# Attention and feed-forward in one kernel: a new written-out order for the steps after the start, another order for the first 300

## The chip, the cores and the metric

The kernel runs on one core of a Trainium2 chip. The metric is the device time of one execution in microseconds (us); "before" is the kernel as it was, "after" the changed one.

## The reference, cut to what matters

Batch 8, 12 heads, 448 rows, head width 64. The attention output, with the heads side by side, is the 3584 x 768 input of a two-layer feed-forward block of width 2048. Inputs and output are f32.

```
q_n = q / sqrt(mean(q*q) + 1e-6) * g_q          # k_n in the same way
attn = softmax(q_n @ k_n^T / 8);  x = attn @ v  # (8, 12, 448, 64) -> (3584, 768)
h = x @ w_in                                    # (3584, 2048)
out = (h * clip(h + 3, 0, 6) / 6) @ w_out       # (3584, 768)
```

## The kernel before

Two heads of one batch form a pair, and there are 48 pairs, six to a batch. For each pair the kernel loads q, k and v (`ld`, 256 KB each, from SyncE's queue; k and q of a pair go into one tile `qk`), squares q and k (`sq`, or `sqh` for half of a q), sums the squares (`red1`, `red15`, `redh`, `red2`), takes the inverse root as a logarithm and an exponential (`ln`, `ex`), scales q and k into `qks` (`sc`, or `sch` for half of a q), casts v into `va` (`cv`), transposes `qks` (`tr`, `trh` on TensorE with the copies `ck`, `cq`, `cqh`; later pairs by DMA and the scaling `kt`), multiplies for the scores (`s`), takes their exponential (`e`), multiplies by v (`av`, `avh`), divides by the row sum (`rd`, `xn`, `xnh`) and transposes the result into `xT` (`xt`, `xth` with `cx`, `cxh`, or a DMA). Batch 0 is worked in two halves of its rows, so that its first scores can start early.

When a batch's six pairs are done, its hidden columns follow: `h1`, `h3` multiply `xT` by `w_in_sb`, `relu` (ScalarE, into `ts`) and `gate` (VectorE, into `gT`) make the activation. The last product (`y384`) is done for pairs of row tiles with seven products in place of eight, for which sums and differences of `gT` (`ga`, 128 x 1024 bf16, two inputs in SBUF) and of `w_out_sb` (`wb`) are formed, and the parts of `y` are added up (`yt`, `yu`, `cy384`) and stored. The weights come in eight DMAs from GpSimd's queue: `w_in` in four column strips (strip c of four is read by the hidden columns 4c to 4c+3), `w_out` in four row strips.

The kernel doesn't run these loops as they stand. Each operation is put into a plan as a numbered step with its predecessors and the engines that may do it; the loops only make the list of 2487 steps. Two tables written out by hand then decide everything: `ORDER` lists the step numbers in the order in which they are issued, and `WAY` names, for steps that have a choice, which of their engines does it (0, the first, where it has no entry). `em` ties every instruction to the one before it on its engine, so each engine works through its own steps strictly in the order of `ORDER`, and a step whose input is late holds up all later steps of its engine.

```
for i in order:
    kind, engines, fn, preds = self.ops[i]
    fn(engines[WAY.get(i, 0)])
```

So the k-th instruction of an engine in the trace can be matched with the k-th step that `ORDER` gives to that engine; step numbers beside trace times below come from this. At line 635 and 657 stand the exponentials, at 399 and 401 the squares (ScalarE, GpSimd), at 404 the scaling by the root, at 385, 387 and 389 the copies and casts (ScalarE, VectorE, GpSimd), at 869 the sums `ga`, at 838 the sums `wb`, at 1008 the DMAs of `w_in`, at 889 the last product, at 769 the gate.

Of the kernel before, what the change touches and what calls it, by code (L numbers as in the profile page):

```python
# [24 lines left out]
    53: 1, 54: 1, 61: 1, 63: 2, 68: 1, 69: 1, 83: 1, 84: 1, 90: 2, 95: 1, 121: 1, 122: 1, 126: 1, 127: 1,  # L25
    128: 1, 145: 1, 150: 1, 151: 1, 158: 1, 160: 1, 209: 1, 215: 1, 216: 1, 227: 1, 234: 1, 245: 1, 247: 1,
    335: 1, 336: 1, 365: 2, 386: 1, 456: 1, 461: 1, 473: 1, 488: 1, 489: 1, 522: 1, 553: 1, 570: 1, 588: 2,
    605: 1, 617: 1, 623: 2, 634: 1, 636: 1, 652: 2, 663: 1, 736: 1, 779: 1, 785: 1, 796: 1, 804: 1, 805: 1,
    837: 2, 863: 1, 880: 1, 888: 1, 889: 1, 895: 2, 926: 1, 927: 1, 991: 1, 998: 1, 999: 1, 1066: 1, 1092:
    1, 1107: 2, 1118: 1, 1133: 1, 1150: 1, 1165: 2, 1185: 1, 1191: 2, 1223: 1, 1226: 1, 1230: 1, 1231: 1,  # L30
    1303: 1, 1316: 1, 1319: 1, 1320: 1, 1326: 1, 1343: 1, 1358: 1, 1377: 1, 1378: 1, 1384: 2, 1395: 1, 1404:
    1, 1427: 1, 1435: 1, 1500: 1, 1535: 1, 1536: 1, 1563: 1, 1564: 1, 1567: 1, 1572: 1, 1575: 1, 1599: 1,
    1616: 1, 1622: 2, 1639: 1, 1647: 1, 1665: 1, 1673: 1, 1680: 1, 1699: 1, 1738: 2, 1757: 1, 1764: 2, 1775:
    1, 1795: 1, 1810: 1, 1811: 1, 1839: 1, 1871: 1, 1876: 1, 1889: 1, 1899: 1, 1925: 1, 1931: 2, 1942: 1,
    1951: 1, 1957: 2, 1968: 1, 1976: 1, 1977: 1, 1983: 1, 2000: 1, 2015: 2, 2047: 1, 2071: 1, 2076: 1, 2079:
    1, 2082: 1, 2083: 1, 2103: 1, 2131: 1, 2135: 1, 2139: 1, 2143: 1, 2146: 1, 2147: 1, 2183: 1, 2212: 1,
    2219: 1, 2236: 1, 2250: 1, 2271: 1, 2325: 1, 2340: 1, 2381: 1, 2413: 1, 2421: 1, 2434: 1, 2442: 1, 2445:
    1, 2448: 1, 2453: 1, 2454: 1, 2484: 1,
# [4 lines left out]
    58, 57, 35, 68, 92, 61, 36, 59, 12, 70, 60, 29, 69, 62, 209, 15, 73, 71, 211, 64, 72, 119, 74, 240, 37,  # L43
    83, 30, 66, 210, 76, 38, 39, 118, 65, 84, 40, 75, 67, 41, 227, 85, 18, 102, 77, 104, 103, 93, 42, 94,
    79, 212, 81, 43, 222, 80, 86, 44, 95, 45, 82, 87, 221, 105, 96, 129, 88, 46, 258, 19, 122, 228, 131,
    121, 89, 224, 47, 63, 48, 97, 49, 229, 120, 98, 106, 130, 110, 111, 223, 99, 107, 108, 112, 230, 132,
    113, 109, 114, 100, 123, 153, 213, 50, 145, 51, 146, 133, 115, 154, 243, 245, 135, 52, 147, 148, 78,
    134, 241, 116, 244, 214, 155, 367, 101, 239, 342, 149, 136, 215, 124, 247, 137, 226, 156, 246, 345, 150,
    0, 336, 248, 216, 344, 128, 231, 169, 225, 335, 232, 392, 152, 117, 90, 171, 242, 257, 151, 233, 138, 1,
    161, 249, 2, 495, 139, 162, 250, 140, 395, 358, 3, 368, 163, 164, 125, 126, 170, 127, 157, 159, 141,  # L50
    142, 337, 160, 158, 143, 144, 172, 175, 187, 185, 173, 386, 338, 176, 217, 177, 165, 166, 188, 167, 174,
    218, 178, 179, 168, 199, 180, 219, 186, 181, 251, 339, 197, 200, 234, 189, 366, 190, 182, 183, 191, 301,
    192, 220, 184, 198, 193, 201, 299, 235, 202, 194, 252, 195, 203, 236, 302, 196, 300, 313, 204, 314, 205,
    206, 237, 303, 385, 238, 365, 311, 312, 325, 253, 326, 304, 340, 305, 207, 254, 306, 208, 323, 307, 315,
    348, 267, 387, 268, 324, 349, 316, 308, 359, 317, 318, 319, 341, 346, 309, 269, 371, 310, 347, 255, 327,
    328, 320, 321, 372, 360, 329, 270, 369, 370, 488, 256, 330, 375, 271, 322, 331, 562, 259, 350, 332, 376,
    351, 352, 361, 353, 362, 364, 260, 363, 333, 354, 343, 489, 393, 373, 334, 398, 377, 374, 378, 396, 497,
    261, 379, 531, 355, 262, 399, 263, 402, 397, 356, 380, 490, 381, 264, 357, 388, 394, 265, 400, 403, 491,
    272, 404, 524, 405, 401, 389, 406, 501, 266, 273, 382, 499, 502, 523, 407, 275, 408, 276, 507, 409, 500,
    390, 277, 492, 505, 383, 274, 279, 410, 384, 494, 280, 391, 506, 278, 511, 411, 561, 508, 503, 281, 512,  # L60
    493, 283, 504, 553, 513, 284, 514, 285, 509, 510, 534, 536, 282, 287, 288, 515, 535, 286, 516, 517, 518,
    537, 289, 540, 291, 292, 525, 519, 520, 290, 521, 542, 293, 582, 541, 522, 295, 526, 543, 496, 532, 527,
    296, 581, 294, 4, 538, 565, 5, 563, 539, 412, 413, 528, 414, 415, 544, 545, 546, 547, 297, 564, 583,
    416, 298, 566, 417, 529, 420, 421, 569, 548, 418, 422, 549, 570, 552, 550, 551, 6, 571, 419, 423, 424,
    554, 425, 645, 592, 426, 567, 428, 572, 568, 429, 555, 573, 593, 430, 574, 575, 7, 530, 556, 576, 594,
    427, 577, 598, 432, 578, 579, 431, 646, 595, 616, 433, 580, 584, 585, 557, 596, 436, 647, 437, 617, 559,
# [12 lines left out]
    838, 871, 849, 685, 688, 842, 847, 827, 850, 828, 845, 875, 686, 689, 1075, 846, 687, 690, 894, 692,
    837, 691, 851, 693, 893, 852, 696, 855, 1076, 694, 848, 697, 698, 876, 856, 695, 854, 867, 857, 858,  # L80
    859, 700, 860, 701, 877, 896, 836, 699, 702, 901, 873, 703, 874, 704, 705, 878, 708, 1077, 899, 881,
    706, 882, 1045, 709, 829, 902, 774, 707, 905, 883, 771, 710, 879, 711, 926, 884, 1046, 1078, 1065, 811,
    1048, 712, 900, 713, 714, 885, 861, 1127, 716, 886, 717, 715, 880, 788, 903, 839, 1055, 718, 1053, 719,
    904, 720, 721, 907, 908, 909, 910, 814, 1054, 722, 1056, 906, 870, 869, 724, 723, 1101, 1100, 911, 1047,
    912, 725, 1059, 1061, 1057, 1126, 1066, 726, 1060, 474, 728, 727, 887, 913, 729, 1128, 475, 1058, 730,
    732, 897, 731, 733, 1129, 1063, 734, 840, 1085, 914, 735, 1064, 915, 918, 919, 916, 920, 1102, 1080,
    917, 921, 1062, 1067, 1068, 922, 1091, 1079, 927, 1069, 1070, 1049, 1086, 935, 928, 923, 1103, 1130,
    1071, 487, 929, 1072, 1111, 1092, 1089, 1159, 1087, 486, 930, 934, 924, 1117, 776, 936, 1083, 1090,
    1158, 1051, 1112, 1104, 925, 937, 1073, 1132, 1160, 1050, 1088, 1135, 938, 931, 932, 872, 1093, 1094,
    1320, 1095, 895, 933, 1161, 1096, 1081, 939, 1097, 1185, 1184, 1098, 1106, 940, 942, 1109, 1115, 1113,  # L90
    1118, 1116, 943, 944, 1186, 1105, 941, 1119, 947, 777, 945, 948, 1114, 1120, 1187, 946, 1108, 1137,
# [1068 lines left out]
```

## Time and profile before

| | us |
|---|---|
| median of 3 runs (lowest, highest) | 421.85 (421.47, 422.01) |
| the profiled execution | 422.05 |
| its span, first to last instruction | 420.3 |
| TensorE busy in it | 403.0 |
| VectorE, ScalarE, GpSimd busy | 294.1, 290.3, 242.4 |
| TensorE's mean granted clock | 0.988 |

The span is 1.75 us shorter than the execution's own time. PE is TensorE, PEld its weight loads, DVE VectorE, ACT ScalarE, POOL GpSimd, SP SyncE. Rows of groups end with busy time and the mean duration of one in ns; a row of the timeline begins with its start and its duration in us, and `[x <-y]` is the idle time before it and who ended that.

### The profile page before, as it was taken

Reading aid. Unit: us, or ns where it says so; the run is one execution under the profiler, and the core shown is the slowest. Engines: PE = TensorE matmul, PEld = TensorE weight load, DVE = VectorE, ACT = ScalarE, POOL = GpSimd, SP = SyncE. Lnnn points to the kernel's source line nnn. Section 1 sums busy time; section 2 is a strip of 40 time slices with the busy share of each in tenths; the row PEclk is TensorE's granted clock in tenths of the full one; section 3 lists DMA queues with packets and bytes.
Section 4 is the critical chain, followed back from the end, with each engine's and each line's share of the span. In section 5 each row is a group of like instructions: output and inputs, shape, how many; then the busy total and the mean of one; then the engine's idle time right before and its main releaser. Section 6 shows DMA issues by size and latency. Waiting matters only on the chain.

```text
span 420.3 us, 9978 instructions
## 1 busy us (share of the span) xinstructions
PE 403.0 (96%) x3872; PEld 236.6 (56%) x3872; DVE 294.1 (70%) x542; ACT 290.3 (69%) x533; POOL 242.4 (58%) x225
## 2 busy tenths in 40 slices
PE   7679999999999999999999999989999999999986
PEld 3356788655454556455555555645555555555644
DVE  4977788599779775685858788776666454565673
ACT  6968989888898886779877786768665764324000
POOL 3584788589697695694857649483244461120230
PEclk9968999999999999999999999999999999999999
DMA  7999979987758795679387369693063641120234
GB/s 247 349 308 246 249 171 218 288 191 191 127 163 229 189 193 154 167 212 236 96 210 210 82 163 257 137 241 84 0 162 78 82 118 24 36 76 2 75 76 113
DMA packets 98979, 67.76 MB, mean 161 GB/s; under 512 B 53204, under 2 KB 95476, under 8 KB 98932
## 3 DMA queue, kind: packets, MB, share of 16 engines
q1 hardware_dynamic: 93488, 60.69, 56.6%
q0 software_dynamic: 5248, 6.29, 8.7%
q8 instruction: 30, 0.49, 0.5%
q14 instruction: 17, 0.14, 0.1%
q10 hardware_dynamic: 196, 0.15, 0.1%
HBM read 50.23 MB, written 11.01 MB: 146 GB/s over the span
## 4 chain that ended last, share of the span: by engine, by line
PE 86%; DVE 5%; DMA 4%; ACT 2%; issue 1%; SPq 1%; POOL 1%; DVEq 0%; POOLq 0%; ACTq 0%
PE M L813 27%; PE M L889 24%; PE X L715 9%; PE S L629 6%; PE M L794 5%; PE S L889 4%; PE X L629 3%; DMA qk<-in_k_dram 2%; DVE gT L869 2%; DMA gT<-in_q_dram 1%; PE S L813 1%; PE XF L674 1%; PE S L652 1%; PE X L889 1%; PE X L813 1%
## 5 line engine op out<-in xcount | busy, mean ns | idle before, releaser
L813 PE MATMUL M<-xT,w_in_sb 128*128 128x448 bf16 x618 | 133.0, 353 | 0.0
L635 ACT ACTIVATE eT<-S 112x896 bf16<-112x896 f32 x112 | 100.6, 917 | 9.2 <-PE S L629 8.9
L404 POOL TENSOR_TENSOR qks<-qk,rs 112x512 bf16<-112x512 f32 (+1 forms) x81 | 87.9, 1098 | 30.4 <-ACT rs L468 20.9
L769 DVE SCALAR_TENSOR_TENSOR gT<-ts,M 128x448 bf16<-128x448 f32 x119 | 73.0, 616 | 42.2 <-ACT ts L766 41.7
L766 ACT ACTIVATE ts<-M 128x448 f32<-128x448 f32 x119 | 64.8, 545 | 51.8 <-PE M L813 42.4
L813 PEld LDWEIGHTS <-w_in_sb 128*128 128x128 bf16 x672 | 60.8, 98 | 58.4 <-issue 10.7
L889 PEld LDWEIGHTS <-gT 128*128 128x128 bf16 x592 | 54.5, 98 | 44.9 <-issue 9.6
L889 PE MATMUL M<-w_out_sb,gT 128*128 128x384 bf16 (+1 forms) x392 | 71.2, 324 | 2.6 <-DVE gT L769 2.4
L401 POOL TENSOR_TENSOR sq<-qk 112x512 f32<-112x512 f32 (+1 forms) x48 | 53.7, 1128 | 23.2 <-DVE ssq L489 7.4
L635 ACT ACTIVATE eT<-X 112x896 bf16<-112x896 f32 x56 | 51.4, 917 | 15.3 <-PE X L629 12.7
L715 PEld LDWEIGHTS <-eT 112*128 112x128 bf16 x1344 | 50.4, 97 | 11.4 <-issue 0.9
L489 DVE TENSOR_REDUCE ssq<-sq 112x16 f32<-112x1024 f32 x42 | 50.7, 1210 | 3.2 <-ACT sq L399 3.2
L715 PE MATMUL X<-va,eT 112*128 112x65 bf16 x1344 | 52.8, 194 | 0.0
L869 POOL TENSOR_TENSOR ga<-gT 128x1024 bf16<-128x1024 bf16 x12 | 26.2, 2181 | 18.1 <-PE M L889 9.0
L629 PE MATMUL S<-T 64*128 64x448 bf16 x224 | 34.5, 353 | 0.0
L869 POOL TENSOR_TENSOR gT<-gT 128x1024 bf16<-128x1024 bf16 x11 | 24.1, 2193 | 14.6 <-DVE ga L869 13.8
L918 POOL TENSOR_TENSOR y<-y 128x384 f32<-128x384 f32 x9 | 9.0, 999 | 40.4 <-DVE y L918 33.4
L913 DVE TENSOR_TENSOR y<-M,y 128x384 f32<-128x384 f32 x37 | 20.4, 552 | 16.4 <-PE M L889 12.3
L734 DVE TENSOR_TENSOR xn<-X,rd 112x512 bf16<-112x512 f32 x42 | 29.0, 690 | 2.0 <-DMA xT<-xn 0.9
L889 PEld LDWEIGHTS <-ga 128*128 128x128 bf16 x232 | 21.7, 98 | 14.1 <-issue 0.7
L889 PE MATMUL M<-wb,ga 128*128 128x384 bf16 x152 | 28.7, 326 | 0.0
L629 PEld LDWEIGHTS <-T 64*128 64x128 bf16 x336 | 12.2, 94 | 24.9 <-issue 19.8
(115 smaller groups left out, 508.4 us busy)
## 6 DMA issues: line engine op xcount, KB each, us to landing
qk<-in_k_dram SPq DMA_DIRECT2D x41, 256.0 KB, 3.9
qk<-in_q_dram SPq DMA_DIRECT2D x41, 256.0 KB, 4.2
vf<-in_v_dram SPq DMA_DIRECT2D x37, 256.0 KB, 4.5
w_in_sb<-in_moe_w_in_dram POOLq DMA_DIRECT2D x4, 768.0 KB, 17.5
w_out_sb<-in_moe_w_out_dram POOLq DMA_DIRECT2D x4, 768.0 KB, 10.1
out_dram<-y SPq DMA_DIRECT2D x8, 336.0 KB, 2.9
out_dram<-y SPq DMA_DIRECT2D x8, 288.0 KB, 3.6
out_dram<-y SPq DMA_DIRECT2D x7, 240.0 KB, 3.6
```

The source lines that it names most:

```text
L401: em(nc.gpsimd.tensor_tensor(out=out, in0=in_, in1=in_, op=A_MULT))
L404: em((nc.vector if e == DVE else nc.gpsimd).tensor_tensor(out=out, in0=in_, in1=by.unsqueeze(3).to_broadcast(list(in_.shape)), op=A_MULT))
L489: em(nc.vector.tensor_reduce(out=ssq[:].rearrange("p i n -> p (i n)"), in_=sq[:].rearrange("p i (n d) -> p (i n) d", d=D), axis=AX_X, op=A ...
L629: em(nc.tensor.matmul(out=ps[:, a, 0:S], lhsT=qkT[r, S + t * TP:S + t * TP + 128], rhs=qkT[r, 0:S], start=True, stop=True))
L635: em(nc.scalar.activation(out=eT[:, t, 0:S2].rearrange("p (a s) -> p a s", a=2), in_=ps[0:TP, :, 0:S], func=EXP, bias=0.0, scale=1.0))
L715: em(nc.tensor.matmul(out=X_ps[:, a, i * E1:(i + 1) * E1], lhsT=eT[:, t, c:c + 128], rhs=va[:, a, t, :], start=(t == 0 and i == 0), stop=( ...
L734: em(nc.vector.tensor_tensor(out=xn[:].rearrange("p i a d -> p a i d"), in0=view()[:, :, :, 0:D], in1=rd[:].unsqueeze(3).to_broadcast([TP, ...
L766: em(nc.scalar.activation(out=ts[:], in_=ps()[:, 0:S], func=RELU, bias=0.5, scale=1.0 / 6.0))
L769: em(nc.vector.scalar_tensor_tensor(out=out, in0=shape(ts[:]), scalar=1.0, in1=shape(ps()[:, 0:S]), op0=A_MIN, op1=A_MULT))
L813: em(nc.tensor.matmul(out=ps()[:, 0:S], lhsT=w_in_sb[:, kt, f * 128:(f + 1) * 128], rhs=xT[:, kt, :], start=(kt == 0), stop=(kt == NKT - 1)))
L869: em((nc.vector if e == DVE else nc.gpsimd).tensor_tensor(out=out, in0=rows(*x), in1=rows(*y), op=op))
L889: em(nc.tensor.matmul(out=ps()[:, 0:nc0], lhsT=lhs[f], rhs=rhs[f][:, c0:c0 + nc0], start=(start and f == 0), stop=(f == HF - 1), skip_grou ...
```

## The change

Only the two tables differ; the steps, their predecessors, the tiles and all instructions' shapes are the same. In a few words: the order of all steps beyond the first 300 was searched anew, with operations that share VectorE's and GpSimd's ports kept apart, and the first 300 are in the original order. Against the kernel before, the two `ORDER` lists are alike for their first 49 places and differ from there on. The diff's first lines of each table:

```
 WAY = {
-    53: 1, 54: 1, 61: 1, 63: 2, 68: 1, 69: 1, 83: 1, 84: 1, 90: 2, 95: 1, 121: 1, 122: 1, 126: 1, 127: 1,
-    128: 1, 145: 1, 150: 1, 151: 1, 158: 1, 160: 1, 209: 1, 215: 1, 216: 1, 227: 1, 234: 1, 245: 1, 247: 1,
-    335: 1, 336: 1, 365: 2, 386: 1, 456: 1, 461: 1, 473: 1, 488: 1, 489: 1, 522: 1, 553: 1, 570: 1, 588: 2,
...
+    53: 1, 54: 1, 61: 1, 63: 2, 68: 1, 69: 1, 83: 1, 84: 1, 90: 2, 95: 1, 101: 1, 121: 1, 122: 1, 128: 2,
+    145: 1, 152: 2, 209: 1, 227: 1, 245: 1, 310: 1, 334: 1, 365: 2, 385: 1, 456: 1, 473: 1, 480: 1, 489: 1,
+    495: 2, 512: 1, 541: 1, 570: 1, 582: 1, 588: 1, 607: 1, 617: 1, 779: 1, 804: 1, 805: 1, 862: 1, 869: 1,
...
```

Steps that went to another engine, by kind (before -> after): `sc` and `sch` on VectorE 8 -> 1 (on GpSimd 94 -> 101); `sq` and `sqh` on ScalarE 47 -> 44 (GpSimd 55 -> 58); `cv` on VectorE 18 -> 15, on GpSimd 21 -> 24; `ga` on VectorE 35 -> 36, on GpSimd 23 -> 22; `yu` on VectorE 9 -> 13, on GpSimd 13 -> 9; `kt` on ScalarE 19 -> 15; `cy384` on ScalarE 23 -> 20. Of the first 300 places, ScalarE has 63 before and 56 after, VectorE 64 and 63, GpSimd 28 and 34, TensorE 107 and 112.

The queues of ScalarE and GpSimd in the start, from the first place where they part (step:kind):

```
ACT before  154:e 245:sqh 148:ln 214:ex 149:ex 124:ln 247:sqh 156:e 336:sq 128:cv 231:ln 335:sq 232:ex 249:ln
            250:ex 125:ex 170:e 160:cqh 158:ck 172:e 386:sq 338:ln 188:e 186:e 339:ex 200:e 198:e 302:e 300:e
            314:e 312:e 326:e 324:e 349:e 347:e 372:e ...
ACT after   154:e 124:ln 214:ex 231:ln 125:ex 156:e 170:e 148:ln 232:ex 149:ex 172:e 101:cv 245:sqh 186:e
            188:e 198:e 200:e 300:e 249:ln 302:e 312:e 250:ex 314:e 324:e 338:ln 339:ex 326:e 347:e 349:e ...
POOL before 78:cv 101:cv 342:cv 0:w_in 392:cv 152:cv 233:sch 1:w_in 2:w_in 495:cv 358:sq 3:w_in 251:sch 252:sch
            385:sq 340:sc 359:sq 341:sc 364:sc 363:sc 524:sq 523:sq 390:sc 494:sc 391:sc 493:sc ...
POOL after  78:cv 0:w_in 126:sc 127:sch 150:sc 151:sch 215:sch 216:sch 233:sch 247:sqh 336:sq 234:sch 358:sq
            335:sq 251:sch 252:sch 1:w_in 359:sq 2:w_in 340:sc 342:cv 341:sc 386:sq 363:sc 364:sc 3:w_in 523:sq
            488:sq 390:sc 524:sq 391:sc 494:sc 493:sc ...
```

On SyncE's queue the load 240 (k of pair 8) stands 14th before and 31st after, and load 257 (q of pair 10), which overwrites what step 216 reads, stands 35th before and 23rd after.

289 rows, old and new, of tables (ORDER, WAY) are left out of this document.

## The prediction

> **What bounds the kernel now.** I read the page's totals, clock line and chain first, then a table by stage.
>
> ```profile
> PE 403.0 (96%) x3872; PEld 236.6 (56%) x3872; DVE 294.1 (70%) x542; ACT 290.3 (69%) x533; POOL 242.4 (58%) x225
> PEclk9968999999999999999999999999999999999999
> 0.00:10.00 10.00, 7.51 (x36) 3.14 (x37) 4.70 (x20) 6.03 (x18) 3.38 (x15) 1.00 0.77 241
> 10.00:20.00 10.00, 7.15 (x81) 3.78 (x80) 9.04 (x23) 9.03 (x23) 6.30 (x9) 1.00 1.10 350
> 20.00:30.00 10.00, 7.38 (x104) 5.29 (x103) 7.14 (x18) 7.94 (x18) 7.29 (x10) 0.66 1.13 322
> 30.00:40.00 10.00, 8.58 (x134) 6.10 (x135) 6.83 (x22) 7.09 (x10) 6.46 (x8) 0.83 1.18 245
> 50.00:400.00 350.00, 347.01 (x3265) 200.47 (x3265) 247.12 (x424) 248.65 (x446) 209.07 (x177) 1.00 0.62 148
> 400.00:421.00 21.00, 15.33 (x110) 9.91 (x107) 10.92 (x16) 1.75 (x4) 3.52 (x2) 1.00 0.35 94
> ```
>
> The columns after the stretch and its length are busy us of PE, PEld, DVE, ACT and POOL, then granted clock, share of the DMA engines and GB/s. From 50 to 400 us TensorE is busy for 347.01 of 350 us: it is the bound, and an order cannot shorten its own work, because the change leaves its instructions as they are. What an order can win lies in the first 40 us, where TensorE is busy for 30.6 us (the sum of the four rows) and partly at half clock (0.66, 0.83), in the few waits later, and in the tail.
>
> In the first 40 us I looked for the queue that TensorE waits for. ScalarE's timeline shows it; after the exponential at 15.39 (step 154) it does work that scores don't wait for:
>
> ```profile
> 15.39 0.92 ACT L657 ACTIVATE eT<-S 112x896 bf16<-112x896 f32 x1
> 18.01 0.40 ACT L399 ACTIVATE sq<-gT 112x256 f32<-112x256 f32 x1
> 19.12 0.62 ACT L399 ACTIVATE sq<-wb 112x512 f32<-112x512 f32 x1
> 19.64 0.61 ACT L385 CAST gT<-xT 112x512 bf16<-112x512 f32 x1
> 20.25 0.62 ACT L399 ACTIVATE sq<-wb 112x512 f32<-112x512 f32 x1
> 23.35 0.34 ACT L385 COPY gT<-M 128x224 bf16<-128x224 bf16 x1 [1.13 <-PE M L577]
> 23.59 0.64 ACT L393 ACTIVATE gT<-M,gp_t 128x448 bf16<-128x448 bf16 x1
> 24.12 0.92 ACT L657 ACTIVATE eT<-S 112x896 bf16<-112x896 f32 x1
> 24.91 0.64 ACT L399 ACTIVATE sq<-wb 112x512 f32<-112x512 f32 x1
> 36.56 4.31 ACT L657 ACTIVATE eT<-S 112x896 bf16<-112x896 f32 x5
> ```
>
> The exponential at 24.12 is step 172, whose score stood ready long before. The last row holds steps 326, 324, 349, 347 and 372, 0.86 us apart, so step 347 begins at 39.1. I take it as the mark for the end of the start: both orders put nearly the same TensorE steps ahead of it (after: one score and one `avh` fewer, two `h1` and one `trh` more).
>
> **Part 1, the first 300 steps.** The change takes the steps of the rows at 18.01, 19.12, 20.25 and 24.91 (247, 336, 335, 386) to GpSimd and those at 19.64, 23.35 and 23.59 (128, 160, 158) to VectorE. Costs of one:
>
> ```profile
> L657 ACT ACTIVATE eT<-S 112x896 bf16<-112x896 f32 x24 | 21.0, 911 | 3.9 <-PE S L652 3.6
> L465 ACT ACTIVATE rs<-ssq 112x12 f32<-112x12 f32 x4 | 0.8, 202 | 0.9 <-DVE ssq L523 0.9
> L404 POOL TENSOR_TENSOR qks<-qk,rs x81: 612/1042/2302, 7.5 to 330.7; 112x512 bf16<-112x512 f32 x77, 112x256 bf16<-112x256 f32 x4
> L401 POOL TENSOR_TENSOR sq<-qk x48: 612/1039/2811, 8.1 to 313.5; 112x512 f32<-112x512 f32 x46, 112x256 f32<-112x256 f32 x2
> L1008 POOL DMA_DIRECT2D w_in_sb<-in_moe_w_in_dram x4: 826/882/1015, 24.3 to 30.3; - x4
> 16.48 0.61 POOL L389 CAST gT<-vf 112x512 bf16<-112x512 f32 x1
> 50.62 1.04 POOL L404 TENSOR_TENSOR qks<-qk,rs 112x512 bf16<-112x512 f32 x1
> ```
>
> *ScalarE's bound.* The two queues are alike up to step 154, so that again begins at 15.39. From there to step 347 the new queue holds 14 exponentials at 0.911, 11 roots at 0.202, one cast (0.61) and one half square (0.40): 12.75 + 2.22 + 1.01 = 16.0 us, and 347 could begin at 31.4; with 0.4 us for a score that is late, 31.8. That is 7.3 us ahead of 39.1. Of the 7.3, the seven steps above are 3.87 us, one exponential less 0.91, and the rest is waiting.
>
> *GpSimd's bound.* The cast at 16.48 (step 78) ends at 17.09 in both. Behind it the new queue reaches the scaling of step 493 after 9 scalings (1.042), 8 squares (1.039), 9 half ones (0.612), one cast and 4 `w_in` issues (0.882): 9.38 + 8.31 + 5.51 + 0.61 + 3.53 = 27.3, so at 44.4 if it never waits. The last row is step 493 before: 50.62. This queue allows a lead of 6.2 us, less than ScalarE's, and it is the one that decides. The Trainium skill (GPSIMD Engine Reference, section "Performance versus the Vector engine") says that elementwise work belongs on VectorE, GpSimd being roughly twice as slow, so it speaks against these moves. By that rule the start would be paced by GpSimd, as this sum has it; the trace's 1.042 against 0.691 us for the same scaling (the row is below) makes the ratio 1.5.
>
> *What takes from the 6.2.* First, step 386 there squares k of pair 8, and its load now stands 31st on SyncE's queue. Ahead of it lie 31 loads of 0.262 MB and two strips of 0.786 MB, 9.7 MB. The GB/s of the first four rows bring 2.4, 5.9, 9.1 and 11.6 MB by 10, 20, 30 and 40 us, so it lands near 32.4; with a third strip, near 35.5. GpSimd asks for it after 21 steps of the list, 17.1 us, at 34.2: a wait of 0 to 1.3, I take 0.6. Load 257 waits for step 216 (near 22.5) and everything behind it on SyncE's queue with it; those loads are in the count. Second, the clock. TensorE lost (0.34 + 0.17) x 10 = 5.1 us of full clock between 20 and 40 us. With more work in this stretch it may keep the clock, which the sums above assume; if it doesn't, I estimate half of the 5.1 on the path, 2.6. I take 1.1, nearer to none because the new queues leave fewer gaps. So the lead is 6.2 - 0.6 - 1.1 = **4.5 us**, with ends at 2.3 (6.2 - 1.3 - 2.6) and 7.3. After the mark TensorE is dense, and the lead stays.
>
> VectorE gets three casts and two copies in this stretch and gives away seven scalings (0.691 or, for half a q, less); it has 63 steps there in place of 64, so I cost that at nothing. Its cover is that it waits for TensorE and ScalarE there anyway.
>
> **Part 2, the other 2187 steps.** TensorE's waits after 40 us, their longest two in the timeline, and the operations that cause them:
>
> ```profile
> PE M L889 <- DVE gT L769: 2.4, 2, 1.6
> PE M L889 <- DVE gT L869: 1.6, 1, 1.6
> 276.47 3.22 DVE L869 TENSOR_TENSOR gT<-gT 128x1024 bf16<-128x1024 bf16 x1
> 277.03 2.12 POOL L869 TENSOR_TENSOR ga<-gT 128x1024 bf16<-128x1024 bf16 x1
> 280.28 0.97 PE L889 MATMUL M<-w_out_sb,gT 128*128 128x384 bf16 x5 [1.61 <-DVE gT L769]
> 401.87 3.69 DVE L869 TENSOR_TENSOR gT<-gT 128x1024 bf16<-128x1024 bf16 x2
> 402.45 2.56 POOL L869 TENSOR_TENSOR gT<-gT 128x1024 bf16<-128x1024 bf16 x1
> 405.62 0.82 PE L889 MATMUL M<-wb,gT 128*128 128x384 bf16 x4 [1.55 <-DVE gT L869]
> L869 DVE TENSOR_TENSOR ga<-gT x13: 680/691/1620, 156.6 to 411.7; 128x1024 bf16<-128x1024 bf16 x13
> L404 DVE TENSOR_TENSOR qks<-qk,rs x3: 691/691/830, 5.5 to 22.1; 112x512 bf16<-112x512 f32 x2, 112x256 bf16<-112x256 f32 x1
> ```
>
> A sum `ga` alone takes 0.69 us on VectorE; beside GpSimd's it took 3.22, the gate behind it came late, and TensorE stood for 1.61 us. At 402 two of them took 3.69 beside one on GpSimd, and TensorE stood for 1.55. The rule for this is in the Trainium skill (SBUF — State Buffer, section "Who interferes with whom"): a VectorE instruction with two SBUF inputs and a GpSimd one that reads SBUF exclude each other for a whole instruction; 3.22 against 0.69 agrees.
>
> After, step 1803 (the row at 276.47) is on GpSimd behind 1795 and can no longer hold up the gate. At the end 2441 is on GpSimd and 2442 on VectorE behind 2449, so that nothing of GpSimd's stands beside 2449. That is 1.61 + 1.55 = 3.2 us. The third wait (2.4 - 1.6 = 0.8) stays: ahead of the gate 925 stand now 927, 776 and 771, all with two SBUF inputs. A new order has waits of its own that no row shows: its bounds are none (3.2 won) and as many as before had (4.0 by the two rows, so 0.8 lost); I take 0.7, and **2.5 us** won.
>
> By place, keeping apart is only partly done: of VectorE's `wb` and `ga` sums, 20 of 45 overlap a GpSimd step before and 19 of 46 after, when each step is put where TensorE's queue stands at its place.
>
> **Sum.** 422.05 - 4.5 - 2.5 = 415.05 for the profiled execution (span 420.3 and 1.75 around it); the median lies 0.2 lower, so **414.9**. About 0.2%, 0.84 us, is what a measurement of this kernel can tell from no change.
>
> **Rivals.**
>
> *The lead is given back to the weights.* The last `w_in` strip was issued at 30.30 and landed after 24.1 us, at 54.4, just ahead of its first reader.
>
> ```profile
> 30.30 0.88 POOL L1008 DMA_DIRECT2D w_in_sb<-in_moe_w_in_dram  x1
> DMA to landing us min/median/max: 11.3/17.5/24.1
> ```
>
> After, GpSimd issues it near 37.3. With the median 17.5 it lands at 54.8; its reader then stands 3.7 us of TensorE work further back, so 3.6 us of lead remain. If part 2 wins nothing besides, 418.2. For it speaks that the DMA engines are full (1.10 to 1.18); against it that fewer strips are ahead of the last one by then.
>
> *The clock is kept and all waits go:* 422.05 - 7.3 - 4.0, less 0.2: 410.5. The Trainium skill (TensorE: Matmul & The Clock Gate, section on the HAM clock gate) has the clock halved after an idle window of about 3.4 us, and a denser start would avoid that. Here the clock was low in the two rows where ScalarE held TensorE up.
>
> *VectorE becomes the bound, slower than before.* Between 80 and 120 us of TensorE's work the new order gives VectorE 56 instructions in place of 51, among them 8 `wb` in place of 5.
>
> ```profile
> 97.30:138.80 41.50, 40.68 (x419) 22.19 (x418) 34.41 (x57) 37.06 (x70) 34.29 (x29) 1.00 0.74 178
> L838 DVE TENSOR_TENSOR wb<-w_out_sb x6: 943/948/1197, 90.7 to 140.9; 128x1536 bf16<-128x1536 bf16 x6
> ```
>
> Before, it was busy for 34.41 of 41.5 us there. Three more `wb` (2.8) and 0.5 net of the others make 37.7, and ten of its sums can be held by GpSimd. It decides from 0.4 us each (41.5), and costs more than parts 1 and 2 win from 1.1 us each; at 1.4, little over half of what the row at 276.47 lost, it is 37.7 + 14 - 41.5 = 10.2, so 425. Against it: few sums lost that much.
>
> *The change doesn't keep the ports apart:* part 2 is nothing, 417.4.
>
> **Chances.** Forecast 0.45; weights 0.15; ports not apart 0.12; clock and all waits 0.12; no change within 0.84 us 0.04; slower 0.12. Faster by over 0.2% is the sum of the first four, 0.84; same 0.04; slower 0.12. The likeliest case's own range is 411.4 (parts 7.3 and 3.2) to 420.4 (2.3 less 0.8). For 8 in 10 it reaches to 409.5 below, a little past the best case, and to 421.0 above, where the slower cases begin.
>
> **What the profile after would show.** Right: step 172's exponential near 19.5 and step 347's near 33.5; step 493 on GpSimd near 46; clock rows between 20 and 40 us above 0.66 and 0.83; no TensorE wait over 1 us before the two products that waited for 1.61 and 1.55 us. Wrong: GpSimd waiting for a load for over 2 us before step 386, TensorE waiting for the last `w_in` strip, VectorE without idle time between 90 and 135 us, or sums `ga` still above 3 us with a TensorE wait behind them.

## The result, and the profile after

The changed kernel takes 417.19 us (median of 4 runs, 416.05 to 418.70), the kernel before 421.93 (421.47 to 423.10) beside it. The ratio is 0.9886, 95% interval 0.9845 to 0.9927: 4.7 us won. The profiled execution is the fastest of the four, 416.05 us with a span of 414.3.

The totals, the clock line, the table by stage and TensorE's waits from 40 us on, of the changed kernel. Its source is one line shorter, so line 812 is what 813 was before, 868 was 869, and so on.

```profile
PE 399.7 (96%) x3872; PEld 235.4 (57%) x3872; DVE 290.6 (70%) x545; ACT 286.5 (69%) x523; POOL 238.5 (58%) x233
PEclk9999999999999999999999999999999999999999
10.00:20.00 10.00, 9.16 (x127) 5.37 (x125) 9.29 (x27) 9.97 (x26) 9.82 (x14) 1.00 1.11 339
20.00:30.00 10.00, 8.87 (x165) 6.30 (x162) 8.16 (x28) 9.23 (x16) 9.39 (x14) 1.00 1.08 283
30.00:40.00 10.00, 8.92 (x149) 6.52 (x149) 8.61 (x27) 9.13 (x18) 8.87 (x10) 1.00 1.13 230
50.00:400.00 350.00, 344.94 (x3208) 199.41 (x3206) 247.20 (x428) 241.35 (x428) 196.98 (x174) 1.00 0.62 150
PE M L812 <- DVE gT L768: 2.3, 3, 1.5
PE M L793 <- DMA w_in_sb<-in_moe_w_in_dram: 1.6, 2, 1.3
PE M L812 <- DVE y L386: 1.1, 1, 1.1
PE M L888 <- DVE gT L868: 0.4, 1, 0.4
```

Between 10 and 40 us TensorE is busy for 26.95 us instead of 23.11 and the granted clock no longer drops. From 50 to 400 us it is busy for 2.1 us *less* than before. Of the waits from 40 us on, the two long waits behind `ga` are gone, but there are new ones, for three gates (line 768), for a copy of `y`, and for two strips of `w_in` (at 46 and 52 us).

The steps by which the prediction measures the start:

```profile
18.41 0.90 ACT L656 ACTIVATE eT<-S 112x896 bf16<-112x896 f32 x1
28.70 2.51 ACT L656 ACTIVATE eT<-S 112x896 bf16<-112x896 f32 x3
34.51 1.04 POOL L400 TENSOR_TENSOR sq<-wb 112x512 f32<-112x512 f32 x1 [1.09 <-DVE xn L689]
35.51 1.04 POOL L403 TENSOR_TENSOR qks<-wb,rs 112x512 bf16<-112x512 f32 x1
43.39 2.03 POOL L403 TENSOR_TENSOR qks<-qk,rs 112x512 bf16<-112x512 f32 x2
52.30 1.32 PE L793 MATMUL M<-xT,w_in_sb 128*128 128x224 bf16 x12 [1.30 <-DMA w_in_sb<-in_moe_w_in_dram]
```

Step 172's exponential is at 18.41 (24.12 before). The second row holds steps 326, 347 and 349, so 347 begins at 29.5 (39.1). The fifth holds 494 and 493, so 493 begins at 44.4 (50.62).

A better ruler than single steps is the **lead**: TensorE's instructions are matched with the steps, TensorE's work is summed along its queue, and at equal work the two traces are subtracted. It shows where time is won and lost, for this kernel and those of the experiments (us; minus is behind the kernel before):

| TensorE work done | 10 | 22 | 28 | 40 | 100 | 140 | 160 | 250 | 394 (end) |
|---|---|---|---|---|---|---|---|---|---|
| after | 0.1 | 9.4 | 7.6 | 4.6 | 4.7 | 2.8 | 3.2 | 2.9 | 6.3 |
| start alone (first) | 0.2 | 8.7 | -6.8 | -6.8 | -6.7 | -6.7 | -6.6 | -6.6 | -6.6 |
| rest alone (second) | 0.2 | 2.1 | 1.0 | -0.1 | 0.0 | -1.8 | -1.6 | -2.7 | 0.7 |
| start, cast 392 later (fifth) | 0.2 | 9.0 | -0.4 | -0.3 | -0.3 | 0.6 | 0.7 | 0.7 | 0.7 |
| gates first (seventh) | -0.3 | 9.1 | 7.9 | 3.4 | 3.2 | 1.4 | 0.4 | 1.3 | 4.7 |
| loads (eighth) | 0.3 | 8.6 | 7.5 | 6.3 | 5.6 | 3.8 | 4.0 | 3.0 | 6.4 |
| first 640 (ninth) | -0.7 | 8.7 | 7.5 | 1.9 | 0.7 | 1.2 | 1.2 | 1.3 | 1.3 |
| fill (tenth) | -0.2 | 8.1 | 7.0 | 3.3 | 3.7 | 4.3 | 3.4 | 3.5 | 6.9 |
| last version (twelfth) | 0.2 | 7.9 | 6.8 | 5.7 | 5.1 | 4.4 | 3.2 | 4.2 | 7.6 |

So the changed kernel is 9.4 us ahead at 22 us of work, gives more than half of that back by 40 us of work, loses another 1.8 between 100 and 140, and wins 1.8 and 1.4 where the two old waits stood. The experiments ask about each of these.

### The profile page after: what moved, and what is told of

It is laid out like the page before. It is cut to its first block, busy times and chain, and to the rows that moved or that the text cites. A ratio compares the mean times of both kernels' runs of the same rounds, so it can differ in the third digit from the quotient of the medians.

```text
span 414.3 us, 9988 instructions
## 1 busy us (share of the span) xinstructions
PE 399.7 (96%) x3872; PEld 235.4 (57%) x3872; DVE 290.6 (70%) x545; ACT 286.5 (69%) x523; POOL 238.5 (58%) x233
## 4 chain that ended last, share of the span: by engine, by line
PE 80%; DVE 7%; DMA 7%; ACT 2%; issue 1%; SPq 1%; POOL 1%; ACTq 0%; DVEq 0%
PE M L812 26%; PE M L888 24%; PE X L714 9%; PE S L628 5%; PE S L888 4%; DMA w_in_sb<-in_moe_w_in_dram 4%; PE M L793 3%; PE X L628 3%; PE X L888 2%; DMA wb<-in_v_dram 2%; DMA qk<-in_q_dram 1%; PE S L812 1%; DVE wb L837 1%; ACT eT L656 1%; DVE gT L768 1%
## 5 line engine op out<-in xcount | busy, mean ns | idle before, releaser
L888 PEld LDWEIGHTS <-gT 128*128 128x128 bf16 x592 | 54.4, 98 | 39.7 <-issue 5.2
L400 POOL TENSOR_TENSOR sq<-qk 112x512 f32<-112x512 f32 (+1 forms) x47 | 50.4, 1082 | 19.2 <-DMA qk<-in_q_dram 11.5
L714 PEld LDWEIGHTS <-eT 112*128 112x128 bf16 x1344 | 52.1, 97 | 13.0 <-ACT eT L634 0.8
L714 PE MATMUL X<-va,eT 112*128 112x65 bf16 x1344 | 54.9, 193 | 0.0
L868 POOL TENSOR_TENSOR gT<-gT 128x1024 bf16<-128x1024 bf16 x15 | 32.0, 2137 | 16.4 <-DVE ga L868 10.1
L398 ACT ACTIVATE sq<-qk 112x512 f32<-112x512 f32 (+1 forms) x42 | 24.4, 586 | 2.8 <-DMA qk<-in_k_dram 1.8
L793 PE MATMUL M<-xT,w_in_sb 128*128 128x224 bf16 x192 | 22.9, 259 | 1.7 <-DMA w_in_sb<-in_moe_w_in_dram 1.6
```

The costliest lines, as they stand in the source:

```text
L400: em(nc.gpsimd.tensor_tensor(out=out, in0=in_, in1=in_, op=A_MULT))
L714: em(nc.tensor.matmul(out=X_ps[:, a, i * E1:(i + 1) * E1], lhsT=eT[:, t, c:c + 128], rhs=va[:, a, t, :], start=(t == 0 and i == 0), stop=( ...
L793: em(nc.tensor.matmul(out=ps()[:, f * SH:(f + 1) * SH], lhsT=w_in_sb[:, kt, f0:f0 + 128], rhs=xT[:, kt, z * SH:(z + 1) * SH], start=(kt == ...
L868: em((nc.vector if e == DVE else nc.gpsimd).tensor_tensor(out=out, in0=rows(*x), in1=rows(*y), op=op))
L888: em(nc.tensor.matmul(out=ps()[:, 0:nc0], lhsT=lhs[f], rhs=rhs[f][:, c0:c0 + nc0], start=(start and f == 0), stop=(f == HF - 1), skip_grou ...
```

## The experiments

Where an experiment mixes the two orders, the steps that the first list has already issued are left out of the second, and each step keeps the engine of the list that it is taken from, unless said otherwise.

**First to fourth: which part of the change wins.**

```
 first:   after[:300]  + before's others         # the start alone
 second:  before[:300] + after's others          # the rest alone
 third:   before; only the 18 differing engines of the start from after
 fourth:  as the first, all engines as before
```

> The first 300 steps in the changed order and on the changed engines, the other 2187 in the order and on the engines of before. Theory (the start's lead is kept only in part): in the changed kernel's trace TensorE was 9.4 us ahead at 22 us of its work and 4.6 to 4.9 us ahead after the last weight strip, at 40 to 50 us of it. With the rest as before, that lead lasts: 421.9 - 4.7 = 417.2 us (416.6 to 418.2), with the two waits of 1.6 and 1.55 us of before still there. Rival (the start is worth nothing in the end, the rest wins): 421 to 422 us. Rival (the rest of before gives back none of the 9.4, since its steps lie otherwise at the last weight strip): 413 us.

> The first 300 steps as before, the other 2187 in the changed order and on the changed engines. Theory: the two waits of before are gone (+1.8 and +1.4 us of lead in the changed trace) but two gates between 100 and 140 us of TensorE's work come late behind VectorE sums that stand beside GpSimd's (-2.0), so this part alone wins 1.2 us: 420.7 us (420 to 421.5). Rival (the forecast's part 2): 2.5 us won, 419.4 us. Rival (the two parts depend on each other: GpSimd and VectorE have more slack for the new order when they start 6 us earlier): slower than before, 422 to 424 us.

> The order of before throughout; only the 18 steps of the start whose engine differs (four squares and a half square from ScalarE to GpSimd or the other way, three copies from ScalarE to VectorE, seven scalings from VectorE to GpSimd, and so on) take the changed kernel's engine. Theory (ScalarE's queue was the bound, and the relief is what matters): ScalarE has 59 steps instead of 64 up to the exponential of step 347 and loses 3.9 us of other work, which is started at about 35 instead of 39.1 us; at the end 2 to 4 us are left: 418 to 420 us. Rival (the order is what matters: exponentials ahead of work that no score waits for): at most 1 us won, 421 to 422 us. Rival (GpSimd, which gets 44 instead of 37 steps before step 493, becomes the bound in the old order): slower than before, 423 us or more.

> The changed order of the first 300 steps, every step on the engine that it had before; the rest as before. Theory (relief of ScalarE matters): ScalarE keeps all 64 steps up to step 347, so 3.9 us more than in the changed kernel, and 1 us or less is won: 421 to 422 us. Rival (order matters): exponentials come earlier past the squares that stand behind them now, and more than half of the 4.7 us is won: 417.5 to 419.5 us.

Measured: start alone 428.56 us, ratio 1.0157 (1.0121 to 1.0194); rest alone 421.96, 1.0005 (0.9989 to 1.0020); engines alone 433.43, 1.0265 (1.0245 to 1.0285); order alone 428.29, 1.0148 (1.0132 to 1.0164). Neither half wins anything alone, and the start alone costs 6.5 us, though together they win 4.7. No theory had that, only the rival of the second points that way (the parts depend on each other). In the trace of the start alone, GpSimd, VectorE and TensorE:

```profile
34.07 1.03 POOL L400 TENSOR_TENSOR sq<-wb 112x512 f32<-112x512 f32 x1
41.45 0.61 POOL L388 CAST va<-wb 112x512 bf16<-112x512 f32 x1 [6.36 <-DMA vf<-in_v_dram]
43.99 1.22 DVE L488 TENSOR_REDUCE ssq<-sq 112x16 f32<-112x1024 f32 x1 [11.89 <-POOL sq L400]
45.51 0.60 PE L673 MATMUL XF<-gT,eT 112*128 112x65 bf16 x8 [13.44 <-DVE xT L386]
```

The changed start issues the load of v of pair 8 (241) at 30.66 instead of 18.06 us, and it lands at 41.40. The old rest wants it cast by GpSimd (392) at once. Behind the cast waits a square, behind the square VectorE's sum over it, behind that sum a copy that TensorE needs: four queues strictly in order make 13.4 us of idle TensorE out of one late load. In the kernel with the engines alone it is a load again:

```profile
22.98 0.62 POOL L388 CAST va<-wb 112x512 bf16<-112x512 f32 x1 [6.25 <-DMA wb<-in_v_dram]
34.57 1.62 POOL L403 TENSOR_TENSOR qks<-qk,rs 112x512 bf16<-112x512 f32 x2
```

GpSimd stands for 6.25 us before a cast that the old order puts there, and the scaling of step 126, which VectorE had done by 22 us in the kernel before, is issued behind it and runs at 34.57: the rival "GpSimd becomes the bound in the old order" holds, through the place of its steps behind a late load rather than through their work. The order alone has the late cast of the first kernel again (GpSimd waits 3.9 us for its load, TensorE 8.6 behind it).

**Fifth and sixth: the late load taken out of the way.**

```
 order of the first (fifth) or fourth (sixth) kernel:
-    ... 392:cv (GpSimd) third behind the first 300 steps, 562:ld (SyncE) behind it
+    ... 493, 392, 562
```

> As the kernel with the changed start alone, with one step moved: GpSimd's copy of v of pair 8 (step 392, and the load 562 that waits for it) stands behind step 493 instead of third behind the mark. In that kernel's trace load 241, which the changed start issues at 30.66 instead of 18.06 us, landed at 41.40, GpSimd waited 6.4 us for it with the square of step 386's chain behind, and TensorE stood for 13.4 us. Theory (the start wins what the changed kernel kept at its last weight strip, and only the hand-over to the old rest loses it): 422 - 4.7 = 417.3 us (416.5 to 418.5). Rival (the old rest has more such places, since its order counts on the old landing times throughout): the hole is only shortened, 420 to 425 us. Rival (without the new rest's waits at 100 to 140 us even better): 415.5 us.

> The same with every step on the engine that it had before: the order of the start alone, with step 392 later. At 22 us of TensorE's work the kernel with the order alone was 7.8 us ahead, the one with engines and order 8.7. Theory (order matters, engines little): within 1 us of the kernel with both, 417 to 418.5 us. Rival (relief of ScalarE, 3.9 us of work, matters): 419.5 to 422 us.

Measured: 421.81 us, 1.0001 (0.9983 to 1.0020), and 421.76, 1.0015 (0.9997 to 1.0034). The hole is shorter and not gone; the theory of 417.3 falls, the rival (more such places) holds. In the fifth kernel, VectorE and TensorE:

```profile
36.76 1.22 DVE L488 TENSOR_REDUCE ssq<-sq 112x16 f32<-112x1024 f32 x1 [4.93 <-POOL sq L400]
38.28 0.60 PE L673 MATMUL XF<-gT,eT 112*128 112x65 bf16 x8 [6.49 <-DVE xT L386]
```

The old rest wants the sum over the squares 385 and 386 at once too; GpSimd, which the new start gives more to do, has them at 36.7. TensorE is then 9 us ahead of before, but the squares and scalings of later pairs are not. The changed rest puts that sum behind the copies. By the time of the whole kernel, engines and order can't be told apart here, since both versions end where the kernel before does. Ahead of place 300 they can: at 22 us of TensorE's work the order alone is 7.8 us ahead in the fourth kernel's trace and about 6 in the sixth's, engines and order together 8.7 and 9.0 (first, fifth), and the engines alone are 9.8 behind (third). Step 347, at 39.15 us before, begins at 33.86 in the fourth kernel, with a wait of 1.3 us for a load in it, and at 31.55 in the first. So the order makes most of the early lead, and the moved engines make the smaller part.

**Seventh: gates ahead of the sums.** Expected from the changed kernel's trace, where the lead falls at 100 to 140. VectorE, GpSimd and TensorE around the first of these places:

```profile
120.56 2.87 DVE L837 TENSOR_TENSOR wb<-w_out_sb 128x1536 bf16<-128x1536 bf16 x1
123.35 1.14 DVE L768 SCALAR_TENSOR_TENSOR gT<-ts,M 128x448 bf16<-128x448 f32 x2
120.49 2.12 POOL L868 TENSOR_TENSOR ga<-gT 128x1024 bf16<-128x1024 bf16 x1
122.57 1.75 POOL L403 TENSOR_TENSOR qks<-qk,rs 112x512 bf16<-112x512 f32 x1
124.01 0.73 PE L812 MATMUL M<-xT,w_in_sb 128*128 128x448 bf16 x3 [1.46 <-DVE gT L768]
```

```
-    774, ..., 731, ..., 735      777, 942, 938, ..., 941      1499, 1490, ..., 1494      1572, ..., 1571
+    731, ..., 735, 774           938, ..., 941, 777, 942      1490, ..., 1494, 1499      1571, 1572
```

> The changed kernel with five VectorE steps moved: the sums wb 774, wb 777, ga 942 and ga 1499 behind the gates and copies (731 and 735, 938 and 941, 1490 and 1494) that stood behind them, and ga 1571 two places earlier. In the changed trace those four places cost TensorE 1.63, 1.22, 0.84 and 0.57 us, behind sums that took 2.87, 1.48 and 1.53, and 1.77 us beside GpSimd's where 0.95 and 0.69 are usual. Theory (sums held by GpSimd's make the gates late): 3 to 4 us won against the changed kernel, 413.5 us (412.8 to 414.5). Rival (VectorE is short of time there, and what is moved is late elsewhere): 415.5 to 417.5 us.

Measured: 416.64 us, 0.9873 (0.9847 to 0.9899), no different from the changed kernel. The four waits are gone in its trace. In their place the product behind gate 946 waits, one behind `xn` at 128 us, and one (1011) behind a copy of `y` at 167 us:

```profile
137.59 1.82 DVE L837 TENSOR_TENSOR wb<-w_out_sb 128x1536 bf16<-128x1536 bf16 x1
141.73 0.54 PE L812 MATMUL M<-xT,w_in_sb 128*128 128x448 bf16 x2 [1.64 <-DVE gT L768]
```

The sum wb 777, moved behind the copies, is held again (1.82 us), one gate further on. The lead shows that the five moves did not all fare alike. From 100 to 140 us of work it falls as in the changed kernel, so moving 774, 777 and 942 only handed the waits on. From 160 to 250 it rises by 0.9 where the changed kernel loses 0.3, so moving 1499 and 1571 did win. In between, TensorE stands for 1.20 us before the product 1011: the copy that it needs is on VectorE behind step 1343 (`kt`, line 605), which waits 2.61 us for a DMA transposition of `qks`. The time is the rival's. Its reason, that VectorE is short of time, fits the first place, but at 167 us VectorE stands idle for a transfer.

**Eighth: the weights.**

```
 SyncE:   244, 225, 226, 223, 243, 239, 240, 257, 242, 258, ...   (257 waits for step 216; 367 and 496 later)
 GpSimd:  ... 234, 1:w_in, 358 ...                                 (was ... 252, 1:w_in, 359 ...)
```

> The changed kernel with SyncE's and GpSimd's early issues moved: the six loads behind load 257, which waits until 21.6 us, stand ahead of it (225, 226, 223, 243, 239, 240), two loads that nothing needs before 54 us (367, 496) stand later, and the second w_in strip is issued 3.7 us earlier (behind step 234). In the changed trace the strips land at 39.7, 46.0 and 52.3 us, 6.2 us apart, and TensorE waits 1.3 us for the last, where the lead falls from 6.6 to 4.6 us. Theory (the lead is given back to the weight strips): they land 3 to 3.7 us earlier, the wait goes and 1.3 to 2 us are won against the changed kernel: 415 us (414.5 to 416). Rival (while a strip is in flight a load takes 2.1 us instead of 0.72; an earlier strip only makes the loads late): 416.5 to 419 us.

Measured: 416.45 us, 0.9886 (0.9860 to 0.9912). The strips land at 36.0, 42.6 and 49.1 us instead of 39.7, 46.0 and 52.3, TensorE no longer waits for them, and the lead at 40 us of work is 6.3 instead of 4.6. That part of the theory holds. The end does not move: the lead is 5.6 at 100 and 3.8 at 140, and behind gate 691 and ga 1571 TensorE waits 0.3 and 0.6 us longer than in the changed kernel. What is won at the weights is lost at the sums.

**Ninth: the seam at a later place.**

```
 after[:640] + before's others
```

> The changed order and engines for the first 640 steps (to about 67 us of TensorE's work, past the last weight strip of w_in and with the rest that the changed start was searched with), the remaining 1847 steps in the order and on the engines of before. Theory (what the change wins, it wins in the loading phase; the rest of the new order is worth nothing in sum): the lead at that place was 5.0 to 5.3 us in the changed kernel and then lasts, with the two old waits of 1.72 and 1.70 us back and the new ones of 1.62, 1.22 and 0.84 us gone: 421.8 - 5 = 416.8 us (416 to 417.8), no different from the changed kernel. Rival (the forecast's part 2, ports kept apart, wins 2.5 us): this kernel is 2.5 us slower than the changed one, 419 to 420 us.

Measured: 419.07 us, 0.9940 (0.9922 to 0.9958), so 0.5% behind the changed kernel: this speaks for the rival (2.5 us by the rest). But the trace shares it out otherwise. The lead is already 1.9 at 40 us of work, where the two kernels are still alike, because the strips landed later in this execution (the slowest of its six). Its three rows:

```profile
42.39 1.32 PE L793 MATMUL M<-xT,w_in_sb 128*128 128x224 bf16 x12 [1.47 <-DMA w_in_sb<-in_moe_w_in_dram]
48.70 1.32 PE L793 MATMUL M<-xT,w_in_sb 128*128 128x224 bf16 x12 [1.47 <-DMA w_in_sb<-in_moe_w_in_dram]
54.95 1.32 PE L793 MATMUL M<-xT,w_in_sb 128*128 128x224 bf16 x12 [1.31 <-DMA w_in_sb<-in_moe_w_in_dram]
```

Then the seam costs 1.9 us (0.84, 0.73 and 0.33 behind exponentials and one `xn` between 82 and 95 us). From 100 us of work to the end it wins 0.6, the changed kernel 1.6. So the new rest is worth something between 1.0 us (these two traces) and 2.3 (the medians); which of them, these runs leave open.

**Tenth: is it GpSimd that holds the sums?** Six GpSimd steps with two inputs become fills, which leaves part of the result out; nothing else moves:

```
+FILL = (926, 1080, 1131, 1164, 1163, 1507)
     def scale(e, out, in_, by):
+        if plan.fill:                      # set in emit: i in FILL
+            em(nc.gpsimd.memset(out, 0.0)); return
```

> The changed kernel with six GpSimd steps (the sums 926 and 1507, the scalings 1080, 1131, 1164, 1163) replaced by a fill of the same tiles with zeros, so that part of the result is left out; VectorE's queue and every place stay. These are the GpSimd operations with two inputs that ran beside VectorE's wb 774 (2.87 us), wb 777 (1.48), ga 942 (1.53) and ga 1499 (1.77). Theory (two operations with two inputs each, one on VectorE and one on GpSimd, hold each other): those sums take their usual 0.95 and 0.69 us, the waits of 1.62, 1.22 and 0.84 us go, and 3 to 3.7 us are won against the changed kernel, about 414 us. Rival (VectorE is short of time there anyway): the sums are shorter, and TensorE waits for the next gates instead, 416 us or more. Rival (GpSimd's operations do not hold them): durations as before.

Measured: 415.75 us, 0.9865 (0.9848 to 0.9882). The same place as above, VectorE and GpSimd (lines are 5 or 6 further on):

```profile
121.54 0.95 DVE L842 TENSOR_TENSOR wb<-w_out_sb 128x1536 bf16<-128x1536 bf16 x1
122.41 0.61 DVE L773 SCALAR_TENSOR_TENSOR gT<-ts,M 128x448 bf16<-128x448 f32 x1
121.45 0.95 POOL L874 MEMSET ga<- 128x1024 bf16 x1
122.34 0.53 POOL L406 MEMSET qks<- 112x512 bf16 x1
```

The sum takes 0.95 instead of 2.87 us, with GpSimd writing beside it for all of its time. TensorE's waits at gates 731 and 1490 go (1.63 and 0.84 before, the time over a product's own pace), that at copy 938 falls from 1.22 to 0.38, and the lead grows from 3.7 to 4.3 between 100 and 140 where it fell by 1.8. So it is shown that GpSimd's operations hold the sums. The Trainium skill (SBUF — State Buffer, section "Who interferes with whom") states that a VectorE instruction with two SBUF inputs contends with a GpSimd one that reads SBUF and not with one that only writes it; the row with the fill agrees (0.95 beside 0.95). The median did not come to the expected 414: the strips, 1.2 us later in this trace, take from it, and so does a new wait of 1.27 us at 164 us. It is the product 1011 again: the transposition that step 1343 needs lands at 162.96, in the changed kernel at 163.01. TensorE came 1.5 us earlier, and the transfer, though issued 1.5 us earlier too, did not.

**Eleventh: parts put together.** The eighth kernel's first 640 steps, then the old rest with the sums that made its three waits moved:

```
-    776, ..., 925      1803, 1790, ..., 1794      2433, ..., 2441, 2449, 2442 (GpSimd)
+    925, 776           1790, ..., 1794, 1803      2441, 2433, ..., 2449, 2442 (VectorE)
```

> A version out of the parts that the runs have shown: the first 640 steps of the changed order with the loads and the second strip issued earlier (6.3 to 6.8 us ahead at 40 to 67 us of TensorE's work), then the order of before with four VectorE or GpSimd steps moved: wb 776 behind gate 925, ga 1803 behind gates 1790 and 1794, ga 2441 ahead of 2433, ga 2442 from GpSimd to VectorE behind 2449. In the trace of before the three gates and sums cost TensorE 0.93, 1.72 and 1.70 us. Theory (waits of single places add): 421.8 - 6.2 - 3.4 to 4.3 = 411.8 us (411 to 413). Rival (each cured place makes the next one late, as in the kernel with five steps moved): 415 to 416 us.

Measured: 416.14 us, 0.9874 (0.9855 to 0.9893), the rival's time. The wait of 1.72 behind gate 1790 is gone, and at 282 us TensorE waits 2.08 behind a `yt` (1802) that now stands behind 1803. Only the tail's wait is really won (lead 3.3 to 5.0). The seam behind the first 640 steps costs this kernel too: it has the same three waits (0.87, 0.73 and 0.36 us, between 79 and 92 us). TensorE's waits from 54 us:

```profile
PE M L888 <- DVE y L912: 2.3, 2, 1.9
PE X L714 <- ACT eT L634: 0.6, 1, 0.6
PE M L812 <- DVE gT L768: 0.6, 1, 0.6
```

**Twelfth: the sum put where the other engine has time.** What the tenth shows with fills, done with all of the work: GpSimd's ga 926 goes to a stretch in which GpSimd had nothing to do. VectorE's 1499 and 1571 move as in the seventh kernel.

```
 order of the eighth kernel, and:
-    1127, 837, ..., 895, 926, 1080      1499, 1490, ..., 1494      1572, ..., 1571
+    1127, 926, 837, ..., 895, 1080      1490, ..., 1494, 1499      1571, 1572
```

> The changed kernel with the loads and the second strip earlier (as in the kernel with these alone), and three sums moved: GpSimd's ga 926, whose operands are there at 108.9 us, stands behind step 1127, in a stretch in which GpSimd has nothing to do (110.1 to 115.0), instead of at 119.5 beside wb 774; VectorE's ga 1499 stands behind gates 1490 and 1494; ga 1571 two places earlier. Nothing is left out. Theory (sums that hold each other make the gates late, as the kernel with the fill shows): the waits of 1.62, 0.84 and 1.22 us of the kernel with the loads alone go, 2.5 to 3.7 us are won against it: 413.3 us (412.5 to 414.5). Rival (926 holds wb 770 at its new place, or the next gates come late): 415.5 to 417 us.

Measured: 414.28 us (412.33 to 415.02), ratio 0.9807 (0.9781 to 0.9832). It is the best version: 7.4 us faster than before, and its interval ends where that of the changed kernel (0.9845 to 0.9927) has not begun.

```profile
109.84 2.12 POOL L868 TENSOR_TENSOR ga<-gT 128x1024 bf16<-128x1024 bf16 x1
111.50 1.28 DVE L837 TENSOR_TENSOR w_out_sb<-w_out_sb 128x1536 bf16<-128x1536 bf16 x1
111.90 1.34 POOL L388 CAST va<-vf 112x512 bf16<-112x512 f32 x1
120.10 1.78 DVE L837 TENSOR_TENSOR wb<-w_out_sb 128x1536 bf16<-128x1536 bf16 x1
163.18 0.68 DVE L605 TENSOR_SCALAR_CACHE_REDUCE T<-T,gp_t 128x448 bf16<-128x448 bf16 x1 [2.76 <-DMA T<-qks]
164.39 0.92 PE L812 MATMUL M<-xT,w_in_sb 128*128 128x448 bf16 x4 [1.35 <-DVE y L386]
```

At its new place 926 holds a `wb` for only 0.3 us, and wb 774 falls from 2.87 to 1.78 us, held now by the scaling 1080 alone. The wait at gate 731 falls from 1.63 to 0.54, those at 1490 and 1571 are gone. What is left are the copies of `y` at 136 and 164 us (1.22 and 1.51). The second is again the transposition: it is issued at 156.13 instead of 157.68 in the changed kernel and lands at 163.15 instead of 163.01.

Where the gain comes from can be read off the lead, beside the eighth kernel, which has the same loads. From 100 to 140 us of work this one loses 0.7 and the eighth 1.8: the difference of 1.1 is ga 926. From 140 to 160 it loses 1.2 and the eighth gains 0.2: that is the transposition, and the 1.1 is gone. From 160 to 250 it gains 1.0 and the eighth loses 1.0: that is the moves of 1499 and 1571. At the start it is behind the eighth, since in this trace the first reader of the first strip waits 1.61 us. That strip, issued at 16 us as in the changed kernel, lands at 28.89 instead of 24.50, with the second strip and six loads issued earlier. These are single traces, and no kernel has one of the three moves alone.

## Why the prediction was right, and where not

The kernel is faster, as forecast, by 4.7 us and not 7.0: 414.9 us was 2.3 below the median, and the 415.05 for the profiled execution 1.0 below that. Two of the four signs of being wrong came: TensorE waited for the last `w_in` strip, and VectorE was nearly without idle time at the named place (busy for 42.3 of the 45 us from 90 to 135).

*GpSimd's bound, 44.4 if it never waits.* Right to the tenth, and partly by luck: GpSimd waits 1.1 us before step 386 and 0.6 before step 251. The row names VectorE for the 1.1, but the one VectorE step that 386 needs ended at 28.1; what else it needs is load 240, so I take it for the load, inside the 0 to 1.3 foreseen and above the 0.6 taken. Two things make the waits good. Step 78 ended at 16.31 us, 0.8 earlier than the 17.09 that was to hold for both kernels. And one operation starts before the one ahead has ended: steps 386 and 363, of 1.04 us each, start 1.00 apart, which over the 31 steps of the sum comes to about 1.1 us that durations don't see. But this queue did not decide the lead, as the prediction says it does: the 9.4 at the mark went past its 6.2, and of TensorE's waits between 20 and 53 us none is for GpSimd itself (strips 1.6, `xn` 0.9, a copy 0.6, exponentials 0.7).

*ScalarE's bound.* Step 347 began at 29.5, ahead of the bound of 31.4. The same overlap is the reason: three exponentials take 2.51, 0.80 each after the first, where the sum had 0.911. The forecast laid 3.87 of the 7.3 us to the seven steps that ScalarE gives away. The fourth kernel, in which ScalarE keeps them, is 7.8 us ahead at 22 us of work, so most of the early lead comes from putting the exponentials ahead of them.

*The clock.* The 1.1 us taken off for it were not needed; it was granted in full.

*"After the mark TensorE is dense, and the lead stays."* **This is the step that failed.** The lead was 9.4 and not 4.5 at the mark, and it did not stay. Some 3 us of it went by 40 us of work in short waits for exponentials and `xn`, of 0.2 to 0.8 us each, and 1.9 in waits for the last two `w_in` strips (0.43 and 1.46, over a product's own pace). Where the last strip's reader starts as the strip lands, the landing alone fixes what is left, since TensorE stood at that point at 56.81 us before: landings at 52.26 (after), 53.46 (seventh), 53.48 (tenth) and 54.90 (ninth) leave 4.55, 3.35, 3.33 and 1.91. That the two add up to 56.81 follows from how the lead is defined; what the traces show is that the reader starts within 0.05 us of the landing in all four (in the seventh without idle time, since TensorE had stood 1.7 us for the strip ahead of it). So in these kernels the lead beyond 40 us of work is set by the strips, however far ahead the start was. The eighth kernel, in which the strip lands at 49.10 and its reader comes at 50.52 without waiting, keeps 6.3 of its 8.6; there the short waits remain.

This is the mechanism of the first rival, to which I gave 0.15. Its size, 3.6 us left, is near the 4.55 by two errors that partly cancel: the strip landed 2.5 us before the 54.8, and its reader stood 2.1 and not 3.7 us further back than before. That 4.55 equals the forecast's 4.5 is a coincidence too.

*Part 2, 2.5 us.* Both old waits went as foreseen (1.8 and 1.4 in the lead), and so did the 0.8 at gate 925 that was to stay. The mis-sized term is that of the new waits: 0.7 taken, 4.3 measured at four places (1.63, 1.22, 0.84 and 0.57). The price of a held sum stood in the quoted rows, and "only partly done, 19 of 46" as well; I priced the new waits by the waits of the old order and not by those 19. Smaller waits of the old order went too (0.56 behind an `xn` at 183 us and some of 0.3), which the forecast did not count. Of the lead, part 2 brings 1.7 us between 40 us of work and the end; the rest alone (second) 0.7 and nothing by its median.

*VectorE without idle time between 90 and 135.* The third rival named the place, and the price is 1.8 us of lead and not 10: the held sums there lost 1.9, 0.5 and 0.8 us (2.87, 1.48 and 1.53 against 0.95 and 0.69), not 1.4 each for ten. It is not a matter of how much VectorE has to do, since the tenth kernel with the same VectorE queue does not lose it between 100 and 140 us of work.

*The median 0.2 below the profiled execution.* It lay 1.1 above. Between the traces the last strip lands at 52.3 to 54.9 us though it is issued at nearly the same time (37.5 and 37.2 at the ends; the three strips ahead of it 0.7 to 0.8 later in the later trace), and that alone moves the lead by 2.6 us; the other runs of the changed kernel have no trace, so that this is the cause for them too is argued, not shown.

The parts add up for the profiled execution: 4.55 at the strip, 1.72 after it, 0.27 lost behind TensorE's last products, so 6.0 of span.

## What to carry to other kernels

In a kernel whose queues run strictly in a written order, an order can't be valued in pieces: the same 300 steps won 4.7 us with the rest that was searched with them and lost 6.5 with another, because one load that is wanted too early goes through four queues. Where TensorE gets ahead, ask first which transfer it will run into, since all that is won before it is measured at its landing: here a weight strip at 52 us and a transposition at 163 us. A sum that is held by another engine can be cured from either side. Giving the other engine's operation a place where that engine is idle took a gate's wait from 1.63 to 0.54 us. Moving the waiting sum behind the gates in its own queue handed the wait on where VectorE had no idle time, and won at two places later on.

## What the runs showed of the hardware

- A cast on GpSimd, with one input, is held by a VectorE sum with two as well: beside such a sum the cast at 111.90 took 1.34 us, in the eighth kernel 0.61. Gates, with one input in PSUM, were not: the pair at 123.35 in the changed kernel takes 1.14 us together, beside GpSimd's scaling.
- Strips and loads share the DMA engines so that each slows the other. While strips were in flight they landed 6.2 us apart (0.786 MB each) and loads 2.1 us apart, 0.7 otherwise; the stretch from 30 to 40 us moved 230 GB/s, that from 10 to 20, with loads nearly alone, 339. In the third kernel, where the last load ahead landed at 37.18 and the next was issued at 42.35, a strip followed the one before in 3.84 us (40.10 to 43.94). A strip issued at 28.0 landed at 39.7; if it moved in the 6.2 us of the others, which is an estimate, some 5 us passed before it began.
- Issue times within 0.8 us of each other gave landings up to 2.6 us apart, in executions of two kernels that are alike up to there (after and ninth). The transposition for step 1343 landed 5.3 us behind its issue in the changed kernel and 7.0 in the twelfth.
